# Unit 0's rms weights moved from the normalisation to the transposed copies, and head 12 loaded in half rows and transposed by VectorE

## The chip, the cores and the metric

The kernel runs on one core of one Trainium2 chip. The metric is the device time of one execution in microseconds (us), the median of several. PE is TensorE (PEld its weight loads), DVE is VectorE, ACT is ScalarE, POOL is GpSimd, and SP is the engine that issues most DMAs. L410 means line 410 of the kernel before.

## The reference

Attention in which a query sees only the keys of its own cluster, followed by an rms normalisation and a gated feed-forward layer (FFN). There are 4 batches, 8 heads, 768 tokens, head size 64, 16 clusters per head, model width 512 and inner width 1536, all in float32.

```python
q_assign = argmax(einsum('bhsd,hcd->bhsc', q_n, c_n))      # k_assign likewise
mask = q_assign[:, :, :, None] == k_assign[:, :, None, :]
scores = where(mask, scale * q @ k.T, -1e9)
attn = softmax(scores) @ v
x = attn.transpose(0, 2, 1, 3).reshape(B * S, H * D)       # 3072 x 512
xn = x / sqrt(mean(x * x) + 1e-6) * rms_g                   # rms_g: one weight per column
out = (silu(xn @ w_gate) * (xn @ w_val)) @ w_out
```

## The kernel before

**Units.** The work is cut into 8 units, each half a batch: 384 tokens as three tiles of 128. `attention` walks through a unit's 8 heads and three pieces of scores per head. Such a piece is called a gap in the code, since other work is put behind it. A list `fill` holds that other work: the FFN of the unit before (`gv`, alternating gate and val products, L442), the output products of the unit before that (L467), and the preparation of later heads. Each engine executes its instructions in the order written. `spread` mixes two lists evenly by count, and `attention` doles out `fill` by cost over the gaps after the first `skip`. Unit 0 has no FFN to fill with; its gaps take explicit `hooks`, such as the preparation of groups 1 and 2.

**Heads.** Batch and head are numbered together, n = 0 to 31, and four heads make a group g. `trans` brings a head's q and k into transposed form (`qkT`). For n below `BH` the load is one DMA of 192 KB for each of q and k (L88), TensorE transposes 128x128 blocks (L221) and ScalarE or VectorE copies them out of PSUM (L227, L225). For n from `BH` on, four DMAs of 48 KB (L96) bring half rows (32 floats) into place so that one VectorE instruction, which transposes 32x32 blocks, does the rest (L217). `cast` makes the bf16 copies `qext` and `kext`. GpSimd makes those of q (L240); those of k are made by VectorE where a head of group 3 or later is below `BH`, that is, for head 12, and otherwise by GpSimd. Cluster products of TensorE (L254) read `qkT`, and their result is laid under `qext` and `kext` by GpSimd's DMAs (`place`).

**Queues.** SP issues loads in program order. `second_batch`, at gap 14 of unit 0, first sends a small DMA `hold` that waits for unit 0's first results, and behind it queues q and k of heads 12 and 13 and v of heads 8 to 11. `grow`, the rms weights repeated in all 128 partitions, is loaded near the start behind heads 8 to 11 (L585). GpSimd issues the FFN weights (L204, L207).

**Unit 0's normalisation.** At gap 1 of unit 1, `norm` calls `rms(0)`: VectorE squares and sums (L391), takes the root, and multiplies each token tile by its root and by `grow` (L410). GpSimd is held by a one-column copy (`idle`, L685) until that is done. At gap 5 `xtrans_all(0)` has TensorE transpose the three tiles (L425, 12 blocks), VectorE copies three of the four column chunks out of PSUM (L428) and ScalarE the fourth (L430). From gap 6 (`LEAD`) on, the FFN of unit 0 fills unit 1. For later units a DMA transposes instead (L413). Between the two, gaps 2 and 3 of unit 1 carry the transpositions of head 12, the first two entries of `t3`, the list for group 3:

```python
hooks = {(1, 0, 0): late[6], (1, 0, 1): lambda: (late[7](), norm())}
hooks.update({(1, *divmod(2 + i, HT)): t3[i][1] for i in range(n)})
hooks[1, *divmod(LEAD - 1, HT)] = lambda: xtrans_all(0)
fill = spread(ffn[:CUT], prep)
```

`prep` is the preparation that unit 1 carries: group 2's v casts and loads (`c`), its cluster steps (`a`), then group 3's transpositions and casts woven together (`w3`), a load of the output weights, and the first cluster steps of group 3 (`a3`).

Of the kernel before, what the change touches and what calls it, by code (L numbers as in the profile page):

```python
# [9 lines left out]
F32 = mybir.dt.float32  # L10
# [3 lines left out]
ALU = mybir.AluOpType  # L14
ACT = mybir.ActivationFunctionType
# [7 lines left out]
def kernel(  # L23
# [12 lines left out]
    nc = tc.nc  # L36
    B, H, S, D = q.shape
    NC = centroids.shape[1]
    DM = moe_w_gate.shape[0]
    DF = moe_w_gate.shape[1]  # L40
    P = 128
    ST = S // P
    HT = ST // 2
# [5 lines left out]
    CC = DM // P  # L49
    FC = DF // P  # L50
    scale = 1.0 / (D ** 0.5)
# [4 lines left out]
    NQ, NV = 6, 8  # L56
    AV = 4
    LATE = {2: (18, 19, 20, 21), 3: (23, 24, 25), 4: (28, 29)}
    BH = 13
    BG = BH // HG  # L60

    ctx.enter_context(tc.manual_schedule())
    pool = lambda n, b, **kw: ctx.enter_context(tc.tile_pool(name=n, bufs=b, **kw))
    const = pool("const", 1)
# [15 lines left out]
    def src(a, n):  # L80
        b, h = divmod(n, H)
        return a[b, h].rearrange("(p t) d -> p t d", t=ST)

    def load(n, part, on=None):
        if n not in staged:
            staged[n] = stage.tile([P, 2, ST, D], F32, tag="qk", name="qk")
        if n < BH:
            (on or nc.sync).dma_start(out=staged[n][:, part], in_=src((q, k)[part], n))  # L88
            return

        to = staged[n][:, part].rearrange("p t d -> p (t d)").rearrange("p (i r d) -> p i r d", i=HT, d=32)
        of = (q, k)[part][n // H, n % H].rearrange("(r p i e) (c d) -> e c p i r d", p=32, i=HT, e=2, d=32)
        for e in range(2):
            for c in range(2):
                r = 32 * (2 * e + c)
                nc.sync.dma_start(out=to[r:r + 32], in_=of[e, c])  # L96

    def load_qk(n):
        if n < B * H:
            load(n, 0)  # L100
            load(n, 1)

    def load_v(n, vq=None):
        if n >= B * H:
            return
        stagedv[n] = stage.tile([P, ST, D], F32, tag="vs", name="vs", bufs=NV)
        (vq or nc.sync).dma_start(out=stagedv[n], in_=src(v, n))
# [9 lines left out]
    for n in range(2, NQ):  # L117
        load(n, 1)
        load(n, 0)
    grow = const.tile([P, DM], F32)  # L120


    qext = [const.tile([P, HG, S], BF16, name=f"qext{i}") for i in range(4)]
# [82 lines left out]
    def load_o(c):  # L206
        nc.gpsimd.dma_start(out=wo[:, c:c + 4], in_=moe_w_out[c * P:(c + 4) * P].rearrange("(c p) f -> p c f", p=P))  # L207
# [4 lines left out]
    def trans(g, h, part, on=None):  # L212
        if (g, h // 2) not in qkT:
            qkT[g, h // 2] = qk32.tile([P, 2, 2, UQ], F32, tag="qkT", name="qkT")
        qk = staged[g * HG + h]
        if g * HG + h >= BH:
            nc.vector.transpose(qkT[g, h // 2][:, h % 2, part], qk[:, part].rearrange("p t d -> p (t d)"))  # L217
            return
        ps = ps_g.tile([P, UQ], F32, tag="gen", name="tq")
        for i in range(HT):  # L220
            nc.tensor.transpose(ps[:, i * P:(i + 1) * P], qk[:, part, 2 * i:2 * i + 2].rearrange("p t d -> p (t d)"),  # L221
                                ident_f)
        to, by = qkT[g, h // 2][:, h % 2, part], 1.0 / ZS if part and g < BG else 1.0
        if on is nc.vector:
            nc.vector.tensor_scalar_mul(to, ps, by)  # L225
        else:
            nc.scalar.activation(to, ps, ACT.Copy, scale=by)  # L227
# [5 lines left out]
    def cast(on, g, h, part, es=(0, 1)):  # L233
        for e in es:
            to = cols((kext if part else qext)[g % 4][:D, h], g, e)
            of = qkT[g, h // 2][e * D:(e + 1) * D, h % 2, part]
            if on is nc.scalar:
                nc.scalar.copy(to, of)
            else:
                on.tensor_copy(to, of)  # L240
# [136 lines left out]
    xn = {}  # L377
# [3 lines left out]
    by_chunk = lambda a: a.rearrange("p (c x) -> p c x", x=P)  # L381
# [15 lines left out]
    def root(u):  # L397
        nt = UNITS[u][2]
        for t in range(nt):
            squares(u, t, True)  # L400
        ms = small.tile([P, HT], F32, tag="ms", name="ms")
        nc.vector.scalar_tensor_tensor(ms[:, :nt], sq[u][:, 0, :nt], 1e-6, sq[u][:, 1, :nt], op0=ALU.add, op1=ALU.add)
        roots[u] = rsqrt(ms[:, :nt], nt)

    def rms(u):
        if u not in roots:
            root(u)
        x, nt, y = xs[u], UNITS[u][2], roots[u]
        for t in range(nt):
            nc.vector.scalar_tensor_tensor(xn[u][:, :, t], by_chunk(x[:, t]), y[:, t:t + 1], by_chunk(grow), op0=ALU.mult, op1=ALU.mult)  # L410
        if u:
            xnT[u] = xp.tile([P, CC, UQ], BF16, tag="xnT", name="xnT")
            nc.sync.dma_start_transpose(out=xnT[u].rearrange("p c (t x) -> p (c t) x", x=P),  # L413
                                        in_=xn[u].rearrange("p c t x -> p (c t x)"))

    xnT, gvT = {}, {}

    def xtrans_all(u):

        xnT[u] = xp.tile([P, CC, UQ], BF16, tag="xnT", name="xnT")  # L420
        ps = [ps_g.tile([P, 2, UQ], BF16, tag="gen", name="tx") for _ in range(3)]
        to = [ps[(c + 1) // 2][:, (c + 1) % 2] for c in range(CC)]
        for t in range(HT):
            for c in range(CC):
                nc.tensor.transpose(to[c][:, t * P:(t + 1) * P], xn[u][:, c, t], ident)  # L425
        for c in range(CC):
            if c < CC - 1:
                nc.vector.tensor_copy(xnT[u][:, c], to[c])  # L428
            else:
                nc.scalar.copy(xnT[u][:, c], to[c])  # L430

    gates = {}

# [53 lines left out]
    def group_work(g):  # L487

        t, c = [], []
        for h in range(HG):  # L490
            n = g * HG + h
            w = 0.0 if n >= BH else 0.3
            t += [(w, lambda h=h: trans(g, h, 0)), (w, lambda h=h: trans(g, h, 1))]
# [7 lines left out]
            def both(h=h, f=others):  # L501
                cast(nc.gpsimd, g, h, 0)
                f()
                cast(nc.gpsimd if g * HG + h >= BH else nc.vector, g, h, 1, (0,))
            if g == 2:
                c.append((0.0, others))
            else:
                c += [(0.0, both), (0.0, lambda h=h: cast(nc.gpsimd if g * HG + h >= BH else nc.vector, g, h, 1, (1,)))]
        a = []
# [43 lines left out]
    def tokens(g, h, on=None):  # L553
        trans(g, h, 1, on)
        trans(g, h, 0, on)
# [26 lines left out]
        load_v(n)  # L582
    for n in range(H, H + HG):
        load_qk(n)
    nc.sync.dma_start(out=grow, in_=moe_rms_g.unsqueeze(0).broadcast_to([P, DM]))  # L585
    tokens(0, 2)
    casts(pool_, 2, K0, K1, Q0)
    pair_clusters(0, (1,))
# [15 lines left out]
    def second_batch():  # L604
        nc.sync.dma_start(out=hold, in_=invs[0].rearrange("p a t -> p (a t)"))
        for n in range(H + HG, H + NQ):
            load_qk(n)
        for n in range(H, H + AV):
            load_v(n)

    def gap1():
        pair_clusters(1)
        tokens(1, 1)
        casts(pool_, 2, Q1)
        casts(pool_, 3, Q1)
        vcast(2)
        vcast(3)
        head(2)
        head(3)
        casts(pool_, 4, K0, K1, Q0)  # L620
        load_gv(1)
        casts(pool_, 5, K0, K1, Q0)
# [50 lines left out]
    for u in range(1, NU):  # L673
        ffn, o, g = ffn_work(u - 1), out_work(u - 2) if u > 1 else [], u + 2
        if u == 1:
            t, c, a = group_work(2)
            t3, c3, a3 = group_work(3)
            n = LEAD - 4
            w3 = weave(t3[n:], c3)
            prep = c + a + w3[:4] + [(0.0, lambda: load_o(8))] + w3[4:] + a3[:5]  # L680
            idle = const.tile([P, 1], BF16)

            def norm():
                rms(0)
                nc.gpsimd.tensor_copy(idle, xn[0][:, CC - 1, HT - 1, P - 1:])  # L685
                for h in range(HG):
                    casts(pool_, H + h, K0, Q0, K1, Q1)

            hooks = {(1, 0, 0): late[6], (1, 0, 1): lambda: (late[7](), norm())}
            hooks.update({(1, *divmod(2 + i, HT)): t3[i][1] for i in range(n)})  # L690
            hooks[1, *divmod(LEAD - 1, HT)] = lambda: xtrans_all(0)
            fill = spread(ffn[:CUT], prep)
            attention([(1, h) for h in range(H)], fill, LEAD, hooks)
        else:
            fill = ffn_work(u - 2)[CUT:]
            fill = fill[:1] + spread(fill[1:], [(0.0, f) for _, f in (a3[5:] if u == 2 else rest)])
            fill.append((0.0, lambda u=u: rms(u - 1)))
            rows, clusters = group(g)
            fill += [(0.0, lambda n=n: load_qk(n)) for n in LATE.get(u, ())]
            n, m = {2: (8, 4), 3: (12, 4)}.get(u, (len(rows), len(clusters)))  # L700
            fill += spread(o, rows[:n]) + spread(ffn[:CUT], [(0.0, f) for _, f in rows[n:]] + clusters[:m])
            rest = clusters[m:]
            attention([(u, h) for h in range(H)], fill, 1 if g < NG else 0, ahead=1)
# [42 lines left out]
```

## Time and profile before

| what | us |
|---|---|
| median of 3 runs (326.62 to 326.75) | 326.7 |
| the profiled execution | 326.95 |
| its span, first to last instruction | 325.2 |
| TensorE busy | 317.5 |
| VectorE busy | 219.5 |
| ScalarE busy | 245.1 |
| GpSimd busy | 139.2 |

The granted TensorE clock is 0.998 of full speed. Busy times overlap, so they don't add up to the span. What sets the end is read from the chain of waits: the last instruction followed back, at each step to what released it.

### The profile page before, as it was taken

The page shows a single profiled execution, that of the slowest core. Times are in us where ns is not written, and L with a number is a line of the kernel's source. Part 1 is how long each engine was busy: PE and PEld are TensorE (multiplying, and loading weights), DVE is VectorE, ACT ScalarE, POOL GpSimd, SP SyncE. Part 2 cuts the span into 40 slices and gives each one's busy share as a digit, 9 for nine tenths or more (in the row PEclk, how much of TensorE's full clock was granted, in tenths as well). Part 3 has the DMA queues.
Part 4 walks back from the last instruction along what each step waited for, and adds up shares of the span by engine and source line. Part 5 has one row for each costly group of instructions (what it writes and reads, how often), then busy time and mean ns, then how long its engine had stood idle before and what let it go on. Part 6 is the DMA issues. An engine that isn't in the chain of part 4 may idle for free.

```text
span 325.2 us, 7757 instructions
## 1 busy us (share of the span) xinstructions
PE 317.5 (98%) x2833; PEld 190.8 (59%) x2847; DVE 219.5 (68%) x502; ACT 245.1 (75%) x422; POOL 139.2 (43%) x279
## 2 busy tenths in 40 slices
PE   8999899999999999999999999999999999999995
PEld 4546656565656656565566655665566656655654
DVE  5999978888477867688677685876265645681430
ACT  4899988887779777787779867897879868863321
POOL 5999599999642585046917156450000000000000
PEclk9999999999999999999999999999999999999999
DMA  7999995996545654566556440000500040005002
GB/s 254 369 270 176 174 218 108 161 178 168 82 69 119 148 128 75 108 134 143 90 92 131 140 115 34 8 19 1 148 0 2 2 113 34 0 2 144 4 1 98
DMA packets 93223, 34.64 MB, mean 107 GB/s; under 512 B 75136, under 2 KB 90112, under 8 KB 93184
## 3 DMA queue, kind: packets, MB, share of 16 engines
q1 hardware_dynamic: 84016, 27.84, 36.2%
q0 software_dynamic: 8880, 5.91, 11.2%
q8 instruction: 22, 0.36, 0.5%
q10 hardware_dynamic: 288, 0.39, 0.4%
q14 instruction: 17, 0.14, 0.1%
HBM read 28.61 MB, written 6.29 MB: 107 GB/s over the span
## 4 chain that ended last, share of the span: by engine, by line
PE 86%; DVE 9%; ACT 2%; issue 1%; DMA 1%; DVEq 0%; ACTq 0%
PE gate L442 19%; PE val L442 18%; PE o L467 18%; PE s L348 17%; PE acc L366 9%; PE sc L254 3%; DVE kext L332 1%; DVE qext L332 1%; DVE pads L327 1%; DMA boot<-in_centroids_dram 1%; PE o L478 1%; ACT pT L352 1%; DVE qkT L225 1%; DVE xn L391 1%; DVE scT L323 1%
## 5 line engine op out<-in xcount | busy, mean ns | idle before, releaser
L352 ACT ACTIVATE pT<-s,off 128x768 bf16<-128x768 f32 x192 | 170.9, 904 | 30.0 <-PE s L348 29.4
L348 PE MATMUL s<-qext,kext 80*128 80x384 bf16 x384 | 94.8, 327 | 1.6 <-ACT pT L352 0.8
L442 PE MATMUL gate<-xnT,wg 128*128 128x384 bf16 x384 | 78.3, 325 | 0.1
L442 PE MATMUL val<-xnT,wv 128*128 128x384 bf16 x384 | 78.1, 326 | 0.0
L451 DVE SCALAR_TENSOR_TENSOR th<-th,gate 128x384 f32<-128x384 f32 x81 | 44.5, 550 | 33.8 <-ACT th L450 33.4
L467 PE MATMUL o<-wo,gvT 128*128 128x512 bf16 x262 | 66.0, 378 | 0.8
L348 PEld LDWEIGHTS <-kext 80*128 80x128 bf16 x384 | 36.3, 98 | 35.0 <-issue 7.5
L442 PEld LDWEIGHTS <-wg 128*128 128x128 bf16 x384 | 36.2, 97 | 23.6 <-issue 0.8
L455 DVE SCALAR_TENSOR_TENSOR gvT<-th,val 128x384 bf16<-128x384 f32 x81 | 44.4, 549 | 8.3 <-PE val L442 3.1
L366 PEld LDWEIGHTS <-pT 128*128 128x128 bf16 x1152 | 43.4, 97 | 10.1 <-DVE x L373 1.0
L450 ACT ACTIVATE th<-gate 128x384 f32<-128x384 f32 x81 | 39.7, 490 | 12.7 <-PE gate L442 11.9
L442 PEld LDWEIGHTS <-wv 128*128 128x128 bf16 x384 | 35.7, 97 | 22.1
L366 PE MATMUL acc<-vbf,pT 128*128 128x65 bf16 x1152 | 45.7, 193 | 0.6 <-ACT pT L352 0.2
L240 POOL CAST qext<-qkT 64x384 bf16<-64x384 f32 x64 | 35.3, 559 | 19.3 <-DVE qkT L217 9.6
L467 PEld LDWEIGHTS <-gvT 128*128 128x128 bf16 x276 | 26.0, 97 | 26.1 <-issue 0.2
L297 POOL DMA_DIRECT2D qext<-oh x48 | 23.1, 491 | 35.2 <-DVE oh L286 35.2
L240 POOL CAST kext<-qkT 64x384 bf16<-64x384 f32 x60 | 33.0, 549 | 4.6 <-DVE qkT L225 2.4
L297 POOL DMA_DIRECT2D kext<-oh x48 | 23.1, 488 | 13.3 <-DVE oh L286 12.3
L470 ACT COPY o_sb<-o 128x512 f32<-128x512 f32 x23 | 13.5, 585 | 17.6 <-PE o L467 17.6
L371 DVE RECIPROCAL inv<-acc 128x6 f32<-128x6 f32 x32 | 6.0, 189 | 25.1 <-PE acc L366 24.6
L217 DVE STREAM_TRANSPOSE qkT<-qk 128x384 f32<-128x384 f32 x38 | 19.5, 553 | 0.0
L373 DVE TENSOR_TENSOR x<-acc,inv 128x384 f32<-128x384 f32 x32 | 17.8, 558 | 1.1
(79 smaller groups left out, 226.6 us busy)
## 6 DMA issues: line engine op xcount, KB each, us to landing
vs<-in_v_dram SPq DMA_DIRECT2D x32, 192.0 KB, 4.1
out_dram<-o_sb SPq DMA_DIRECT2D x23, 256.0 KB, 2.5
qk<-in_q_dram SPq DMA_DIRECT2D x76, 48.0 KB, 2.8
qk<-in_k_dram SPq DMA_DIRECT2D x76, 48.0 KB, 2.5
qk<-in_q_dram SPq DMA_DIRECT2D x13, 192.0 KB, 4.1
qk<-in_k_dram SPq DMA_DIRECT2D x11, 192.0 KB, 4.2
wg<-in_moe_w_gate_dram POOLq DMA_DIRECT2D x4, 384.0 KB, 6.2
wv<-in_moe_w_val_dram POOLq DMA_DIRECT2D x4, 384.0 KB, 8.3
```

Of the source, the lines that this page charges most:

```text
L217: nc.vector.transpose(qkT[g, h // 2][:, h % 2, part], qk[:, part].rearrange("p t d -> p (t d)"))
L240: on.tensor_copy(to, of)
L297: on.dma_start(out=ext[D:D + NC, h, e * UQ:(e + 1) * UQ], in_=put[g, m][32 * h + e * NC:32 * h + (e + 1) * NC])
L348: nc.tensor.matmul(ps[:, j, :w] if nt == HT else flat[:, j * w:(j + 1) * w], lhsT=cols(kext[g % 4][:KR, hh], g, kc // HT, kc % HT * P, (kc ...
L352: nc.scalar.activation(pT[u, h][:, n * i:n * i + n, :w], of, ACT.Exp, bias=off, scale=scale if g >= BG else scale * ZS)
L366: nc.tensor.matmul(acc[:, h % 2, t], lhsT=pT[u, h][:, kc, t * P:(t + 1) * P], rhs=vbf[g % 4][:, hh, kc % HT * 2 + kc // HT], start=kc == 0 ...
L373: nc.vector.tensor_tensor(dst, acc[:, :, :nt, :D], inv[:, :, :nt].unsqueeze(3).broadcast_to([P, 2, nt, D]), op=ALU.mult)
L442: nc.tensor.matmul(ps, lhsT=w[:, c, f * P:(f + 1) * P], rhs=xnT[u][:, c, :n], start=c == 0, stop=c == CC - 1)
L450: nc.scalar.activation(th, ps, ACT.Tanh, scale=0.5)
L451: nc.vector.scalar_tensor_tensor(th, th, 1.0, ps, op0=ALU.add, op1=ALU.mult)
L455: nc.vector.scalar_tensor_tensor(gvT[u][:, f, :n], gates[u], 0.5, ps, op0=ALU.mult, op1=ALU.mult)
L467: nc.tensor.matmul(outs[u], lhsT=gvT[u][:, f, t * P:(t + 1) * P], rhs=wo[:, f], start=f == 0, stop=f == FC - 1)
```

## The change

- `BH` goes from 13 to 12. Head 12's q and k are loaded in half rows, eight DMAs instead of two, and transposed by VectorE. The bf16 copies of its k are made by GpSimd.
- The first two entries of `t3` leave gaps 2 and 3 of unit 1 and go into `prep`, behind `a` and ahead of `w3`.
- For unit 0, `rms` multiplies by the root alone. The weights are applied in `xtrans_all`, where a column of the model lies on a partition: each copy multiplies by a column of `gcol`, a 128x4 tile.
- `gcol` is loaded, element by element, where `grow` was; `grow`, used by units 1 to 7 as before, is loaded at the end of `second_batch`.

```diff
-    BH = 13
+    BH = 12
...
+    gcol = const.tile([P, CC], F32)
...
         for t in range(nt):
-            nc.vector.scalar_tensor_tensor(xn[u][:, :, t], by_chunk(x[:, t]), y[:, t:t + 1], by_chunk(grow), op0=ALU.mult, op1=ALU.mult)
+            if u:
+                nc.vector.scalar_tensor_tensor(xn[u][:, :, t], by_chunk(x[:, t]), y[:, t:t + 1], by_chunk(grow), op0=ALU.mult, op1=ALU.mult)
+            else:
+                nc.vector.tensor_scalar_mul(xn[u][:, :, t], by_chunk(x[:, t]), y[:, t:t + 1])
...
             if c < CC - 1:
-                nc.vector.tensor_copy(xnT[u][:, c], to[c])
+                nc.vector.tensor_scalar_mul(xnT[u][:, c], to[c], gcol[:, c:c + 1])
             else:
-                nc.scalar.copy(xnT[u][:, c], to[c])
+                nc.scalar.activation(xnT[u][:, c], to[c], ACT.Copy, scale=gcol[:, c:c + 1])
...
-    nc.sync.dma_start(out=grow, in_=moe_rms_g.unsqueeze(0).broadcast_to([P, DM]))
+    nc.sync.dma_start(out=gcol, in_=moe_rms_g.rearrange("(c p) -> p c", p=P), allow_slow_non_contiguous=True)
...
         for n in range(H, H + AV):
             load_v(n)
+        nc.sync.dma_start(out=grow, in_=moe_rms_g.unsqueeze(0).broadcast_to([P, DM]))
...
-            prep = c + a + w3[:4] + [(0.0, lambda: load_o(8))] + w3[4:] + a3[:5]
+            prep = c + a + t3[:n] + w3[:4] + [(0.0, lambda: load_o(8))] + w3[4:] + a3[:5]
...
-            hooks.update({(1, *divmod(2 + i, HT)): t3[i][1] for i in range(n)})
```

## The prediction

> **What bounds the kernel now.** I read the busy table first, then the chain of waits in order of time, then each engine's timeline around the one place where the chain leaves TensorE.
>
> ```profile
> PE 317.5 (98%) x2833; PEld 190.8 (59%) x2847; DVE 219.5 (68%) x502; ACT 245.1 (75%) x422; POOL 139.2 (43%) x279
> 42.00:72.00 30.00, 30.00 (x313) 18.01 (x312) 25.14 (x53) 25.40 (x40) 28.25 (x55) 1.00 0.94 168
> ```
>
> TensorE is busy for 98% of the span, and in the window from 42 to 72 us for all 30.00 of 30 us. From 42 us to about 280 us the chain is TensorE's own work with hardly a gap, so nothing that other engines save there can show. Time saved ahead of 42 us shows in full, if TensorE's work after that point stays the same. The chain just ahead of it:
>
> ```profile
> 36.13 0.73 DVE xn L391 x6
> ...
> 38.66 2.09 DVE xn L410 x3
> 40.75 0.05 issue
> 40.80 0.40 PE tx L425 x4
> 41.20 0.34 PE s L348 x2
> 41.54 0.95 PE gate L442 x4
> 42.49 0.65 PE val L442 x4
> ```
>
> Columns are start, length, work. VectorE normalises unit 0's three token tiles (L410), TensorE transposes the last one (L425), and the first gate product waits for the copies. VectorE has no idle time from 28.8 to 40.7 us. TensorE's timeline at the same place:
>
> ```profile
> 36.49 0.49 PE L221 MATMUL tq<-ident_f,qk 128*128 128x128 f32 x3
> 37.06 0.50 PE L348 MATMUL s<-qext,kext 80*128 80x384 bf16 x2
> 37.40 0.49 PE L221 MATMUL tq<-ident_f,qk 128*128 128x128 f32 x3
> 38.23 0.50 PE L348 MATMUL s<-qext,kext 80*128 80x384 bf16 x2 [0.34 <-ACT pT L352]
> 38.57 0.71 PE L366 MATMUL acc<-vbf,pT 128*128 128x65 bf16 x18
> 39.41 0.50 PE L348 MATMUL s<-qext,kext 80*128 80x384 bf16 x2
> 39.75 0.79 PE L425 MATMUL tx<-ident,xn 128*128 128x128 bf16 x8
> 40.80 0.40 PE L425 MATMUL tx<-ident,xn 128*128 128x128 bf16 x4 [0.27 <-DVE xn L410]
> ```
>
> The two L221 rows are head 12's transpositions, about 0.33 us of TensorE each. They fill holes; TensorE waits here for ScalarE's exponentials (at 38.23) and for VectorE (at 40.80). The prices of what goes and comes, from the groups by form (mean ns last before the idle time):
>
> ```profile
> L410 DVE SCALAR_TENSOR_TENSOR xn<-x,n,grow 128x512 bf16<-128x512 f32 x24 | 16.6, 748 | 0.3
> L240 DVE CAST kext<-qkT 64x384 bf16<-64x384 f32 x4 | 1.7, 436 | 0.1
> L428 DVE COPY xnT<-tx 128x384 bf16<-128x384 bf16 x3 | 0.9, 351 | 0.3 <-PE tx L425 0.3
> L187 DVE TENSOR_SCALAR boot<-boot,c_inv 128x64 f32<-128x64 f32 x1 | 0.3, 254 | 0.0
> ```
>
> **What the Trainium skill says.** "VectorE: DVE Perf Modes", the perf-mode tier table: a multiply by a scalar on fp32 data in SBUF makes two results a cycle, an operation with two tensors one; with an operand in PSUM at most two, for 16-bit data. The trace agrees: two-tensor rows of 128x384 take 550 ns, fp32-to-bf16 casts of 384 elements take 340 ns where nothing disturbs them (55.42 us), the bf16 copy out of PSUM 351 ns. "SBUF — State Buffer", who interferes with whom: VectorE in such a two-port mode and GpSimd lock each other out for a whole instruction. The cast at 28.11 us took 0.69 us instead of 0.37 beside GpSimd's casts. During L410 this does not matter: GpSimd waits from 36.8 to 40.9 us for xn (L685). "DMA: Bandwidth & Descriptors", queues, rings and completion order: each DMA engine takes turns between queues by packet, so that a queue of small packets is served slowly beside one of large packets. The trace fits: SP's 48 KB pieces land after a median of 2.6 us, but up to 9.4 us, the longest beside the weight loads between 28 and 44 us.
>
> **Part 1, L410 for unit 0.** Three two-tensor rows of 747 ns, 667 ns apart, become three multiplies by one pointer scalar. From 64 elements (254 ns, L187, with a pointer) 448 more at half of 1.02 ns (the slope between two-tensor rows of 64 and 384 elements, 224 and 550 ns) give 254 + 228 = 482 ns, 0.40 apart since neighbours overlap by 0.08. The last ends at 38.66 + 0.81 + 0.48 = 39.95 instead of 40.74: 0.79 us earlier.
>
> **Part 2, the copies.** Three copies of 351 ns get a pointer. L410's 747 ns against 681 on the same slope prices a pointer at 66 ns, so 0.41 us each, 0.33 apart instead of 0.27. ScalarE's copy (478 ns) grows too; "ScalarE: Activation LUTs", on what ACT_TABLE_LOAD costs, gives 93 ns for a pointer operand, no run here shows it; 0.57 us, taken as an estimate.
>
> **Part 3, head 12 off TensorE and ScalarE.** Six transpositions (0.65 us of TensorE, in holes) and two evictions of 0.49 us (0.38 apart) leave the stretch before L425. ScalarE's next exponentials then run 0.80 us apart instead of 1.16: the one of 38.42 starts at 38.08 and ends at 38.98, so the scores of 39.41 can start at 39.12, when L366 ends. TensorE then transposes tiles 0 and 1 from 39.46 to 40.08, tile 2 from 40.08 (ready at 40.00). The first copy starts at 40.35; copies are done at 40.76, 41.09 and 41.42, ScalarE's by 41.2. The gate's third product starts at 41.48 instead of 42.01, val at 41.80 instead of 42.33. **That is 0.5 us.** If head 12 stayed on TensorE and ScalarE, the transpositions would start at 39.75 and some 0.3 us of it would be lost.
>
> **Part 4, where head 12 goes.** VectorE gets two stream transpositions (L217, 553 ns, 0.49 apart) and loses two casts (0.34 and 0.36 us): +0.4 us between 53 and 60 us. VectorE runs up to 1.3 us behind the products there (val of 54.20 is consumed at 56.17), and TensorE has three PSUM buffers, so it needs them about 1 us after they are freed. Two more items in the list also pull group 2's cluster steps one product earlier, which takes 0.5 us of that lag away. I put the effect at nothing; the cover gone, it is at most 0.4. GpSimd gets two casts of 0.53 us at about 62 us, ahead of the third load of wo. That load is issued at 62.9 and lands within 9.4 us, by 72.3; its first use is near 75.7. One us later is covered.
>
> **Part 5, the queues.** SP issues eight DMAs of 48 KB for head 12 where there were two of 192 KB (0.52 and 0.42 us), ahead of head 13, v 8 to 11, and now grow. In SP's timeline:
>
> ```profile
> 28.48 0.42 SPq L88 DMA_DIRECT2D qk<-in_k_dram  x1
> 28.99 4.04 SPq L96 DMA_DIRECT2D qk<-in_q_dram  x4
> 33.08 3.55 SPq L96 DMA_DIRECT2D qk<-in_k_dram  x4
> 36.73 4.19 SPq L107 DMA_DIRECT2D vs<-in_v_dram  x5
> 42.27 3.45 SPq L96 DMA_DIRECT2D qk<-in_q_dram  x4
> ```
>
> Added issue time is 8 x 0.62 - 0.94 = 4.0 us at the usual 0.62, 6.7 us at the 0.95 seen here. But SP also stands still here, for landings of its earlier DMAs (1.35 us before 42.27), and part of the extra issue falls into that. I take 2 us of delay by head 15's k (issued until 55.0, landing 2.5 later). VectorE wants it about 59.8 us, so 2 us late is still in time; nothing is charged. The v tiles come 1 to 3 us later, GpSimd casts them from 49 us and had 0.6 us to spare at 53.8; what hangs on its queue (cluster rows, wo) is wanted 3 us later or more. At unit 1's own transposition (78.26 us, landing at 82.0, first used at 84.8) SP has been idle for 3.8 us: covered. gcol, 512 elements of 4 bytes, takes grow's place at 16.9 us; SP issues nothing after it until 27.2, and it is first read at 40.3. grow's 256 KB, then issued near 45 us, are first read near 75.
>
> **Sum.** The profiled execution took 326.95 us (span 325.2 and 1.75 around it), 0.25 above the median of 326.7. Its span becomes 324.7, the execution 326.45, and the median **326.2 us**, 0.15% less. A measurement of this kernel can tell about 0.2%, 0.65 us, from no change, so the likeliest outcome lies inside it.
>
> **Rivals.** *More of it arrives* (0.22): if the pointers cost nothing in the copies, whose order leaves VectorE nothing else, 0.2 us more come through: 0.7 us, 326.0; with the transpositions also as early as xn is ready, 0.8, 325.9. For it: VectorE's own gain is 0.79. Against it: three pointers at 66 ns stand in series on VectorE.
>
> *No fast mode* (0.08): if the multiplies run at one element a cycle, L410 keeps its 747 ns, and the copies' 0.18 is a loss: 326.9. If only the copies lose it, they take 0.61 us each and eat the gain: 326.7. The casts at 340 ns speak against the first, the 351 ns copy against the second.
>
> *SP comes late* (0.20, slower): head 15's k lands after VectorE wants it. VectorE executes in order, so the steps behind the waiting transposition wait too (val's product into gvT, th), and TensorE's 16 cluster products at 61.27 read the result directly. Margin: k must be late by over 2.8 us for VectorE to wait, by about 3.3 for TensorE. The full 6.7 us give a stall of 3.4 us, less the 0.5: 329.6. At 4.5 us it is 1.2 - 0.5: 327.4. For it: small pieces here took 0.95 us and landed after up to 9.4. Against it: half of that time SP stands in backlog anyway.
>
> **Numbers.** Chances: my forecast 0.50, the larger gain 0.22, no fast mode 0.08, SP late 0.20. Faster by over 0.2% is the larger gain and a few hundredths of my forecast's spread: 0.25. Same: 0.55, slower 0.20. The likeliest case alone spans 326.0 to 326.4. The range runs from 325.8 to 327.4, the middle of the SP case; its upper half and a little below are left out.
>
> **What would show it.** Right: unit 0's xn multiplies near 0.48 us, the last ending 1.3 us after the first starts; copies near 0.41; the first val product 0.5 us earlier; TensorE gapless from 42 to 72 us. Wrong: multiplies at 0.75 or copies above 0.55; a wait of VectorE's L217 on a DMA, or of L254 on VectorE between 55 and 62 us; a hole in TensorE's row ahead of 80 us; wo products waiting on a load.

## The result and the profile after

| kernel | median us | ratio to before, 95% interval |
|---|---|---|
| before | 326.65 | |
| after | 334.44 (333.94 to 334.62, 5 runs) | 1.0234 (1.022 to 1.0248) |

The change costs 7.8 us, where 0.5 us of gain was forecast. (Ratios leave out executions more than 1.5% above the fastest of their kernel, one each of e2, e3 and e8 below, so that a ratio can be lower than the median suggests.) The lines of the file move by a few: L410 is now L412 for units 1 to 7 and L414 for unit 0, L425 is L429, L428 is L432, L217 is L218, L442 is L446, L254 is L255, L455 is L459. From the page of the kernel after: busy times, the granted TensorE clock in 40 slices, and the group of VectorE's transpositions (busy, mean ns, idle time before them and its cause).

```profile
PE 319.0 (96%) x2841; PEld 190.2 (57%) x2841; DVE 218.9 (66%) x502; ACT 244.5 (74%) x420; POOL 139.3 (42%) x281
PEclk9999999969999999999999999999999999999999
L218 DVE STREAM_TRANSPOSE qkT<-qk 128x384 f32<-128x384 f32 x40 | 20.6, 552 | 7.0 <-DMA qk<-in_k_dram 6.7
```

Two new facts stand in it: VectorE's transpositions wait 7.0 us, nearly all for one load of k, and the ninth slice has a clock of 6 tenths. The chain of waits, in order of time, shows both:

```profile
57.70 8.36 DMA qk<-in_k_dram
66.06 0.03 DVEq L218
66.09 0.05 issue
66.14 0.58 DVE qkT L218
66.71 0.45 DVE gvT L459
67.17 0.04 issue
67.21 1.51 PE sc L255 x8
68.72 0.76 PE s L349 x2
69.47 0.99 PE acc L367 x18
...
72.82 0.65 PE gate L446 x4
...
73.79 0.55 PE acc L367 x18
```

The last of head 15's pieces of k was issued at 57.70 and took 8.36 us to land. VectorE's transposition of it, the next val product into gvT behind it, and TensorE's cluster products follow in a row. From there each row of TensorE is nearly twice as long as its like (acc 0.99 instead of 0.55 at 73.79) until about 72.5 us. TensorE's timeline has the hole itself; its releaser is gvT because the products lacked a free PSUM buffer, which the step behind the waiting transposition frees:

```profile
59.73 0.85 PE L255 MATMUL sc<-qkT,cblk 128*32 128x384 f32 x8
67.21 1.51 PE L255 MATMUL sc<-qkT,cblk 128*32 128x384 f32 x8 [6.63 <-DVE gvT L459]
```

SP's own timeline of the kernel after, from `hold` to head 15's k:

```profile
26.38 0.57 SPq L609 DMA_DIRECT2D hold<-inv  x1
27.05 3.42 SPq L96 DMA_DIRECT2D qk<-in_q_dram  x4
30.52 2.92 SPq L96 DMA_DIRECT2D qk<-in_k_dram  x4
33.55 3.40 SPq L96 DMA_DIRECT2D qk<-in_q_dram  x4
36.99 3.09 SPq L96 DMA_DIRECT2D qk<-in_k_dram  x4
40.18 4.50 SPq L107 DMA_DIRECT2D vs<-in_v_dram  x4
...
53.03 2.62 SPq L96 DMA_DIRECT2D qk<-in_q_dram  x4
55.70 2.91 SPq L96 DMA_DIRECT2D qk<-in_k_dram  x4
```

Head 12 takes eight issues (27.05 to 33.44) where it took two. Head 15's k, issued from 52.38 to 55.0 before, goes out from 55.70 to 58.6. GpSimd issues the first two loads of the output weights at 55.74 and 56.5, before it is through. SP's row and GpSimd's row before, then GpSimd's after:

```profile
52.38 2.63 SPq L96 DMA_DIRECT2D qk<-in_k_dram  x4
57.75 1.58 POOL L207 DMA_DIRECT2D wo<-in_moe_w_out_dram  x2
```

```profile
55.74 1.57 POOL L208 DMA_DIRECT2D wo<-in_moe_w_out_dram  x2
```

So the order is turned round. Before, the four pieces of k landed 2.4 to 3.1 us after their issue; after, those issued at 55.7, 56.4, 57.0 and 57.7 landed after 2.7, 6.2, 8.3 and 8.4 us.

The place where the gain was forecast, in VectorE's timeline:

```profile
37.81 1.28 DVE L414 TENSOR_SCALAR xn<-x,n 128x512 bf16<-128x512 f32 x3
39.42 1.07 DVE L432 TENSOR_SCALAR xnT<-tx,gcol 128x384 bf16<-128x384 bf16 x3 [0.33 <-PE tx L429]
```

and in TensorE's:

```profile
38.61 0.93 PE L429 MATMUL tx<-ident,xn 128*128 128x128 bf16 x12
39.38 0.51 PE L349 MATMUL s<-qext,kext 80*128 80x384 bf16 x2
39.89 1.14 PE L446 MATMUL gate<-xnT,wg 128*128 128x384 bf16 x4
40.86 0.81 PE L446 MATMUL val<-xnT,wv 128*128 128x384 bf16 x4
```

Three multiplies take 1.28 us instead of 2.08, three copies 1.07 instead of 0.89, and TensorE no longer waits for the last token tile. From the first multiply to the first val product it is 3.05 us, where it was 3.67 (38.66 to 42.33). Distances are compared here, not times: this execution reached the first multiply 0.85 us earlier than the profiled one of before, and it was ahead by 0.4 us already at 3.1 us, when VectorE began with the centroids.

### The profile page after: what moved, and what is told of

It is laid out like the page before. It is cut to its first block, busy times and chain, and to the rows that moved or that the text cites. A ratio compares the mean times of both kernels' runs of the same rounds, so it can differ in the third digit from the quotient of the medians.

```text
span 332.7 us, 7769 instructions
## 1 busy us (share of the span) xinstructions
PE 319.0 (96%) x2841; PEld 190.2 (57%) x2841; DVE 218.9 (66%) x502; ACT 244.5 (74%) x420; POOL 139.3 (42%) x281
## 4 chain that ended last, share of the span: by engine, by line
PE 85%; DVE 6%; ACT 4%; DMA 3%; SPq 1%; issue 1%; POOL 0%; DVEq 0%; ACTq 0%; POOLq 0%
PE o L471 18%; PE val L446 18%; PE gate L446 18%; PE s L349 16%; PE acc L367 9%; ACT pT L353 3%; PE sc L255 3%; DMA qk<-in_k_dram 3%; SPq L96 1%; PE warm L133 1%; DVE pads L328 1%; DVE kext L333 1%; DVE qext L333 1%; PE o L482 1%; DVE scT L324 1%
## 5 line engine op out<-in xcount | busy, mean ns | idle before, releaser
L446 PE MATMUL val<-xnT,wv 128*128 128x384 bf16 x384 | 78.8, 328 | 0.0
L446 PE MATMUL gate<-xnT,wg 128*128 128x384 bf16 x384 | 78.4, 325 | 0.1
L471 PE MATMUL o<-wo,gvT 128*128 128x512 bf16 x276 | 67.7, 379 | 0.0
L455 DVE SCALAR_TENSOR_TENSOR th<-th,gate 128x384 f32<-128x384 f32 x81 | 44.6, 550 | 34.1 <-ACT th L454 33.8
L459 DVE SCALAR_TENSOR_TENSOR gvT<-th,val 128x384 bf16<-128x384 f32 x81 | 44.4, 548 | 9.9 <-PE val L446 4.8
L446 PEld LDWEIGHTS <-wg 128*128 128x128 bf16 x384 | 36.2, 97 | 23.9 <-issue 1.2
L446 PEld LDWEIGHTS <-wv 128*128 128x128 bf16 x384 | 35.9, 98 | 22.5 <-issue 0.7
L218 DVE STREAM_TRANSPOSE qkT<-qk 128x384 f32<-128x384 f32 x40 | 20.6, 552 | 7.0 <-DMA qk<-in_k_dram 6.7
```

Source lines behind the costliest of these rows:

```text
L446: nc.tensor.matmul(ps, lhsT=w[:, c, f * P:(f + 1) * P], rhs=xnT[u][:, c, :n], start=c == 0, stop=c == CC - 1)
L455: nc.vector.scalar_tensor_tensor(th, th, 1.0, ps, op0=ALU.add, op1=ALU.mult)
L459: nc.vector.scalar_tensor_tensor(gvT[u][:, f, :n], gates[u], 0.5, ps, op0=ALU.mult, op1=ALU.mult)
L471: nc.tensor.matmul(outs[u], lhsT=gvT[u][:, f, t * P:(t + 1) * P], rhs=wo[:, f], start=f == 0, stop=f == FC - 1)
```

## The experiments

The theory after the result (A): the whole loss is head 15's k landing late; it lands late since its last pieces share the DMA engines with the output weights' loads; and the clock adds to the stall. Rivals: the weights' part costs time too (B), SP's delay alone does it (C), half rows of head 12 hurt wherever they are loaded (D), the slow products have another cause than the stall (E), the freed engines help by themselves (F), grow's place is what delays SP (G).

**e1, the weights' part alone.**

```diff
-    BH = 12
+    BH = 13
...
+            hooks.update({(1, *divmod(2 + i, HT)): t3[i][1] for i in range(n)})
```

(and `prep` without `t3[:n]`)

> The weights' part alone: gcol and the multiplying copies, head 12 as before on TensorE and ScalarE. Theory A (all of the loss is head 15's k landing late behind the output weights' loads, and that comes from head 12's half rows): no wait of a transposition on a DMA, no loss; 0.2 to 0.3 us faster than before, 326.4, since TensorE can't start the transpositions of xn ahead of 39.75. Rival B (the weights' part costs time too, by gcol or by grow's later load): slower than before by 0.5 us or more.

Measured: 325.95 us, ratio 0.9985 (0.9973 to 0.9998). No transposition waits for a DMA. First multiply to first val product: 38.11 to 41.44, 3.33 us, so 0.34 us gained. B falls: this part alone costs nothing.

**e2, head 12's part alone.** The kernel before with `BH = 12`, `t3[:n]` in `prep` and no such hooks.

> Head 12's part alone: half rows, VectorE's transpositions in the list; weights and grow as before. Theory A: nearly the whole loss, 333 to 335 us, with one wait of 5 to 7 us of a VectorE transposition for head 15's k. Rival B (part of the loss is the weights' part or grow's place in the queue): clearly less, below 331.

Measured: 331.92 us over six runs from 328.87 to 334.44, ratio 1.0139 (1.0095 to 1.0182). Its profiled execution is the longest of them, with a span of 332.7 us, and has VectorE waiting for head 15's k; the row is VectorE's:

```profile
65.62 0.58 DVE L217 STREAM_TRANSPOSE qkT<-qk 128x384 f32<-128x384 f32 x1 [5.65 <-DMA qk<-in_k_dram]
```

The wait is there without the weights' part. The median is lower than A said, and by the ratio (331.0 us) the loss is at the edge of what B said, though e1 shows that the weights' part costs nothing alone. What that part adds fits a race: counted from VectorE's first multiply (L410, L414), the output weights are issued after 18.73 us here and after 17.93 in the kernel after, mostly since the gain brings them forward; k's last piece goes out 1.0 us behind them here and 2.0 there. No run tests this by itself. The spread is wide where the kernel before stays close together: what is lost differs from execution to execution.

**e3, the output weights later.** The changed kernel, two loads moved on GpSimd's queue.

```diff
-(0.0, lambda: place(nc.gpsimd, g, 1)), (0.0, lambda: load_o(0)), (0.0, lambda: load_o(4)),
+(0.0, lambda: place(nc.gpsimd, g, 1)), (0.0, lambda: None), (0.0, lambda: None),
...
-w3[:4] + [(0.0, lambda: load_o(8))] + w3[4:]
+w3[:4] + [(0.0, lambda: [load_o(c) for c in (0, 4, 8)])] + w3[4:]
```

> The changed kernel with the first two loads of the output weights moved some 5 us later on GpSimd's queue, next to the third. Theory A (k of head 15 lands late because these loads share the DMA engines with it): k lands within 4 us of its issue, VectorE waits at most 2 us for it, 326.5 to 329 us; the output products may now wait for their weights by up to 2 us. Rival C (SP's issue alone is too late, the output weights don't matter): the wait stays at 6 to 7 us, 333 to 335.

Measured: 327.94 us (327.12 to 332.57), ratio 1.0052 (1.0035 to 1.0069). SP issues head 15's k even later than in the kernel after, at 56.76 instead of 55.70. VectorE's rows:

```profile
58.75 0.58 DVE L218 STREAM_TRANSPOSE qkT<-qk 128x384 f32<-128x384 f32 x1 [0.27 <-DMA qk<-in_q_dram]
61.37 0.58 DVE L218 STREAM_TRANSPOSE qkT<-qk 128x384 f32<-128x384 f32 x1 [0.90 <-DMA qk<-in_k_dram]
```

The wait shrinks from 6.66 to 0.90 us, TensorE's from 6.63 to 0.83, and the clock stays at 1.00. C falls as the cause of the whole loss: late issue alone costs TensorE 0.83 us, and the landing behind the output weights the rest. The moved loads have a price of their own, at another place than expected: a load of v issued at 66.15 takes 8.96 us to land, GpSimd waits for it, and rows of `kext` come so late that TensorE stands another 0.89 us at 84.42. The two waits are 1.7 of the 2.1 us that this execution loses between the first val product and the last output products (278.84 us, 276.75 before).

**e4, head 12 loaded earlier.** The changed kernel, with head 12's eight loads behind those of heads 8 to 11, where SP was idle.

```diff
-    for n in range(H, H + HG):
+    for n in range(H, H + HG + 1):
         load_qk(n)
...
-        for n in range(H + HG, H + NQ):
+        for n in range(H + HG + 1, H + NQ):
```

> The changed kernel with head 12's eight loads put behind those of heads 8 to 11, ahead of gcol, where SP has ten idle microseconds. Theory A: SP reaches head 15's k as early as in the kernel before or earlier, no wait on a DMA; only the gain of 0.5 to 0.6 us is left: 326.1. Rival C: the same. Rival D (half rows of head 12 hurt wherever they are loaded, by slowing the weight loads that run at that time): slower than before by 1 us or more.

Measured: 325.54 us, ratio 0.9969 (0.9958 to 0.998). No transposition of VectorE waits for a DMA, and TensorE is busy for all 30.00 us from 42 to 72. From the first multiply to the first val product it is 3.05 us (38.20 to 41.25), as in the kernel after. D falls. This version is faster than both kernels.

**e5, TensorE kept busy in the stall.** The changed kernel with 29 products of no use ahead of group 3's cluster products.

```diff
+            w0, f0 = a3[0]
+            a3[0] = (w0, lambda: (hot(29), f0()))
```

(`hot(n)` issues n products of 128x512 into a scores buffer.)

> The changed kernel with 29 idle products of TensorE (some 6.3 us, results unused) ahead of group 3's cluster products, that is, in the stall. Theory A (after 6.6 us of standing still TensorE gets half its clock for some 5 us, which costs 2.4 us on top of the stall): VectorE still waits 6 to 7 us for head 15's k, the granted clock from 66 to 72 us is 1.0 instead of 0.5, and the time falls by about 2.4 us to 332. Rival E (the slow products after the stall come from something else, such as the queue of transfers): clock and time as in the changed kernel, 334.4.

Measured: 332.24 us, ratio 1.0177 (1.0164 to 1.019), 2.2 us less than the kernel after (1.9 by the ratios). The wait is unchanged at 6.76 us. Busy time by stretch, of the kernel after and then of e5; the columns behind the engines are granted clock, DMA share and GB/s:

```profile
60.00:66.00 6.00, 0.58 (x8) 0.00 (x0) 0.00 (x0) 1.41 (x4) 5.56 (x12) 0.97 1.31 214
66.00:72.00 6.00, 4.79 (x34) 2.36 (x35) 2.99 (x6) 2.26 (x5) 3.97 (x9) 0.50 1.07 186
```

```profile
60.00:66.00 6.00, 6.00 (x29) 2.64 (x27) 0.00 (x0) 1.84 (x5) 5.54 (x12) 1.00 1.31 215
66.00:72.00 6.00, 6.00 (x72) 3.17 (x71) 4.59 (x9) 3.35 (x7) 3.30 (x7) 1.00 1.06 184
```

With TensorE kept busy the clock from 66 to 72 us is 1.00 instead of 0.50, at the same DMA load. E falls. The Trainium skill has this in "TensorE: Matmul & The Clock Gate", Part 1: after an idle window of some 3.4 us the array runs at half rate until it has been busy for about as long. The trace agrees on the half rate. The times differ: here the clock fell about 5 us after TensorE had become idle (60.6 to some 65.6) and stayed at half for some 6.8 us, until 72.5, which is 5.3 us after work had resumed at 67.2. And e8 below falls to half clock after a gap of 2.19 us, shorter than the page's window.

**e6, head 12 early, weights as before.** e2 with e4's order of loads.

> Head 12 in half rows, loaded early, on VectorE; the weights as before in L410. Theory A (the chain ahead of the first gate product is VectorE's, and head 12's leaving TensorE and ScalarE only helps once xn comes earlier): within 0.2 us of the kernel before, since xn ends when it did. Rival F (the freed ScalarE and TensorE help by themselves): 0.3 us or more faster than before.

Measured: 326.28 us, ratio 0.9987 (0.9979 to 0.9995). First multiply to first val product: 38.56 to 42.23, 3.67 us, exactly as before, so nothing was gained at that place: F finds no support in the trace, though the time is 0.4 us less (0.16 to 0.69), which is more than A said and would do for F. These 0.4 us lie elsewhere, see below.

**e7, grow loaded early.** The changed kernel with grow ahead of gcol.

> The changed kernel with grow loaded at its old place ahead of gcol instead of behind v 8 to 11. It takes one DMA of 256 KB out of SP's queue ahead of heads 14 and 15. Theory A (a race between head 15's k and the output weights, decided by a microsecond or two): k is issued about 0.5 to 1 us earlier, the wait shrinks in most executions or varies between them, 328 to 334 us. Rival G (grow's load is the main delay): no wait on a DMA, 326.

Measured: 333.77 us (331.85 to 335.25), ratio 1.0218 (1.0183 to 1.0252), one wait of 5.53 us for head 15's k. Counted from `hold`, k is out 1.3 us earlier than in the kernel after (30.9 us instead of 32.2), and the wait is shorter but stays. grow's place is not the main delay; G falls.

**e8, the output weights earlier, in the kernel before.** Nothing else is changed; SP's queue is as it was.

```diff
-... if m else [(0.0, lambda: place(nc.gpsimd, g, 0, (0,)))]
+... if m else [(0.0, lambda: [place(nc.gpsimd, g, 0, (0,)), load_o(0), load_o(4)])]
```

(and the two later loads taken out)

> The kernel before with nothing changed but the first two loads of the output weights, issued some 5 us earlier on GpSimd's queue. SP's queue is as before. Theory A (those loads starve SP's small pieces): head 15's k, issued as before from 52 to 55 us, lands 3 to 9 us late, VectorE waits 2 to 7 us for it, 329 to 334 us. Rival C (the loss needs SP's own delay): no wait, 326.5 us.

Measured: 329.43 us (327.7 to 332.62), ratio 1.0085 (1.0048 to 1.0122). Its chain of waits:

```profile
53.39 0.62 SPq L96
54.06 8.57 DMA qk<-in_k_dram
62.66 0.02 DVEq L217
```

SP issues head 15's k when it did in the kernel before, by 54.7 us, yet its last piece lands 8.57 us after issue, and VectorE waits 2.51 us for it. GpSimd's first load is issued at 52.78 here; the four pieces, issued at 52.1, 52.7, 53.4 and 54.1, land after 2.6, 2.8, 6.6 and 8.6 us. So the collision makes the wait without any part of the change. C falls a second time.

TensorE stands for 2.19 us, its only wait between 54 and 80 us, and then loses clock all the same (columns as in e5):

```profile
60.00:66.00 6.00, 3.81 (x43) 1.80 (x42) 3.29 (x7) 3.30 (x6) 3.22 (x7) 0.94 1.12 169
66.00:72.00 6.00, 6.00 (x45) 3.40 (x43) 3.28 (x7) 4.88 (x10) 5.59 (x11) 0.78 0.92 146
```

What is missing from a clock of 1.00, (0.06 + 0.22) x 6 us, is some 3.4 us at half clock, which costs 1.7 us. With the 2.19 it makes 3.9 of the 4.0 us that this execution loses between the first val product and the last output products (280.78 us). Of the eight executions, the four from 327.7 to 328.3 us, faster than A said, have a mean clock of 0.999 or more, the four from 330.6 to 332.6 one of 0.988 to 0.995. So clock is lost in some executions and not in others; how long TensorE stands in the shorter ones is not on record.

The ten profiled executions, in us: when the issue of head 15's k was complete, when the first of the output weights' loads was issued, and VectorE's longest wait for k.

| kernel | k issued until | output weights from | wait |
|---|---|---|---|
| before | 55.0 | 57.75 | none |
| e1 | 54.7 | 56.85 | none |
| e6 | 54.4 | 57.30 | none |
| e3 | 59.4 | 61.32 | 0.90 |
| e4 | 55.4 | 56.13 | none |
| e7 | 58.2 | 56.65 | 5.53 |
| e2 | 58.3 | 56.73 | 5.65 |
| e8 | 54.7 | 52.78 | 2.51 |
| e5 | 58.2 | 56.17 | 6.76 |
| after | 58.6 | 55.74 | 6.66 |

Where k is out first, it lands in time or within a microsecond; where the output weights' loads come first, VectorE waits 2.5 to 6.8 us. The kernel before had 2.75 us between the two (e4 gets by with 0.7), in a race that its profile nowhere marks as a wait.

## Why the prediction was wrong

**Parts 1 and 2, the multiplies and copies: right to the hundredth.** Forecast 0.48 us each and 0.40 apart, which is 1.28 us for three; measured 1.28. Copies 0.41 and 0.33 apart, 1.07 for three; measured 1.07. ScalarE's copy, priced from the skill's 93 ns for a pointer: 0.57, and 0.57 was measured.

**Part 3, TensorE and ScalarE freed: right.** Forecast 0.53 us up to the first val product; measured 0.62, most of the surplus being a first copy that starts 0.08 us earlier than forecast. e1 keeps 0.34 us of it and e6 brings 0.00: freeing TensorE and ScalarE adds 0.28 us, and only once xn comes earlier, as argued (some 0.3 us).

**Part 4: right for VectorE.** Without the wait it was not behind; in e4 TensorE has no gap from 42 to 72 us. But the remark that the list pulls group 2's cluster steps one product earlier was not followed to its end: the first two loads of the output weights stand among these steps and moved with them.

**Part 5, the queues: wrong, and this is the step that failed.** The text charged nothing for "2 us of delay by head 15's k (issued until 55.0, landing 2.5 later)". Both terms were too small. The delay of issue was 3.3 us on the clock and 4.2 us measured from the first multiply (13.72 us before, 17.89 after): SP's standing still absorbed less than assumed. That error alone would have cost TensorE about a microsecond (0.83 us in e3). The landing decided: 8.4 us for the last piece, not 2.5. I had written down that a queue of small packets is served slowly beside one of large packets, which is my inference and not the page's sentence, and that SP's pieces had taken up to 9.4 us; then I used the median of all pieces.

The evidence was in the profile before, and I misread it: the 9.4 us are not "beside the weight loads between 28 and 44 us" (there it is up to 9.1) but belong to pieces issued between 62 and 65 us. All pieces issued from 57.7 to 68 us, that is, behind the output weights' loads of 57.75 and 62.89, landed after 3.9 to 9.4 us, 8.1 in the median.

The other side of the race moved as well. Counted from the first multiply, the output weights' loads were issued after 19.09 us before and after 17.93 in the kernel after, 1.16 us earlier: 0.62 us is the gain itself, the rest comes with head 12's entries in the list (e1, without them, has 18.74, its gain alone). Between them, a later k and earlier loads turned 2.75 us ahead into 2.87 us behind.

**A term was missing.** The sum had no price for TensorE's clock after a stall: 2.2 us by e5, and 2.4 us from the chain, where the rows from 67.21 to 72.82 take 5.6 us and their like at full clock 3.2. With it the account closes: -0.62 + 6.63 + 2.4 = +8.4 us; the spans differ by 7.5, and the execution of after was 0.85 us ahead at the first multiply.

**The rival "SP comes late"** named the wait, the instruction behind it and the products that follow it, and said from which delay it decides. Its price was SP's issue time (329.6 at the most) and left out the landing and the clock. It deserved more than a chance of 0.20: the margin of 2.8 us was known (Part 5's own figures, wanted at 59.8 and landed at 57.5, leave only 2.3; in the kernel after VectorE was ready at 59.48), the delay was estimated between 2 and 6.7 us, and I took the low end.

**What stays open.** By their ratios e1, e4 and e6 are faster than before by 0.5, 1.0 and 0.4 us; behind the first multiply the trace locates 0.34, 0.62 and nothing, so 0.15 to 0.4 us are not accounted for. From the first val product to the last output products (L478, L482 there) it is 276.75 us in the profiles of before, e1, e4 and e6 alike. So it lies ahead of the first val product, and outside the stretch from the first multiply to it, where the profiled executions differ in any case: these four reach the first multiply between 38.11 and 38.66 us, the kernel after at 37.81, e3 at 38.84. Whether the moved loads have a part in it, no run here tells.

## What to carry to other kernels

When loads are added to a queue, price not only their issue but the landing of the ones behind them at their new time: look up which large transfers start there, and take the longest landing beside such transfers, not the median. The profile before often has it: here the pieces that already went out behind the output weights. Ask also whether the change moves those large transfers. A load that lands in time shows no wait, so its margin has to be worked out from the next big transfer behind it. A stall of TensorE can cost more than its length, since products after it may run at half clock, here after 6.63 us and in e8 after 2.19; and a kernel with such a stall is repaired by moving the added loads to where their queue is idle, as e4 does for all of the gain.

## What the runs showed of the hardware

- Small pieces from SP (48 KB in half rows of 128 bytes) landed 8.36 us (after) and 8.57 us (e8) after issue when GpSimd's loads of the output weights had been issued at about the same time or before, and after a median of 2.6 us over all pieces of the kernel before; there those issued between 57.7 and 68 us, behind the same loads, took 8.1 in the median. The skill's page "DMA: Bandwidth & Descriptors", queues, rings and completion order, says that the engines take turns between queues by packet; the runs agree in direction, but do not show the packets' turns one by one.
- After 6.6 us without work TensorE ran at a clock of 0.50 for about 5.3 us of renewed work; 29 useless products in the stall kept it at 1.00 and made the kernel about 2 us faster (e5). After 2.19 us without work it ran at half clock for some 3.4 us in the profiled execution of e8.
- On VectorE a multiply of 128x512 float32 values by one scalar per partition took 482 ns (after), where a multiply by such a scalar and a second tensor took 748 (before); a copy of 128x384 bf16 values out of PSUM took 351 ns (before), and 412 with a scalar per partition (after).
